# A fused attention and expert kernel: a new instruction list, sums of four v tokens fetched by an accumulating DMA, and stores issued by SyncE

## The chip, the cores and the metric

One core of one Trainium2 chip runs the kernel. The metric is device time in microseconds. The kernel before took 366.23 us when the change was made (median of three runs, 365.46 to 369.69). Its engines are called as in the profile: PE is TensorE, DVE is VectorE, ACT is ScalarE, POOL is GpSimd, and SP is SyncE. PEld is the loading of weights, which overlaps PE (183.8 us busy beside PE's 351.5 in a span of 367.9).

## The reference

Two kinds of attention are added over 8 batches, 8 heads, 576 tokens and 64 dimensions. One runs over q, k and v averaged by fours and is repeated to full length; the other runs over a band of 7 tokens. The sum, 4608 tokens by 512, goes through a dense pair of products with ELU between.

```python
q_d = q.reshape(B, H, Sd, factor, D).mean(axis=3)      # factor = 4; k_d, v_d alike
out_d = sm_attn(q_d, k_d, v_d)
out_up = np.repeat(out_d, factor, axis=2)
mask = np.abs(pos[:, None] - pos[None, :]) < factor
scores = np.where(mask, scale * q @ k.T, -1e9)          # softmax, then @ v
x = (out_up + out_local)                                # (4608, 512)
h = x @ w_in                                            # (4608, 2048), first product
g = np.where(h > 0, h, np.exp(np.minimum(h, 0)) - 1)
out = g @ w_out                                         # (4608, 512), second product
```

## The kernel before

The kernel is a list of short words, each of which issues some instructions, in an order that was worked out beforehand. Each engine runs its own share of the words in the order of the list. `mm1.t.f` is one block of four matmuls of the first product (0.87 us from start to start). `e`, `m` and `g` are its exponential on ScalarE, its minimum and its final sum on VectorE. `mm2` is the second product, `Tq` and `Tk` turn q and k, `M` multiplies by the band's mask on VectorE, `MUL` scales attention by its denominators on VectorE, `X` adds the two attentions on GpSimd, `C` casts on GpSimd, `L` loads, and `st` stores.

```python
def vsum_mm(b, j, to):                   # averages of 4 v tokens, on TensorE
    for c in range(NB):                  # 6 matmuls
        nc.tensor.matmul(to[0:KG, c // 3, :], at_once("VR")[:, ...], v16[:, c, :, :], ...)
def turn(n, b, j):
    ...                                  # cut
    if n == "q":
        vsum_mm(b, j, to[:, :, GW : GW + 128])
def v_away(b, j):                        # VD: VectorE copies them out of PSUM
    nc.vector.tensor_copy(out=vd[:], in_=x[0:KG])
def masked(b, j):                        # M
    nc.vector.tensor_tensor(out=mex[:], in0=pex[:], in1=mk2, op=AB.mult)
def elu_min(t, fc):                      # m: both operands in SBUF
    nc.vector.tensor_scalar(out=e[:], in0=e[:], scalar1=1.0, scalar2=-1.0,
                            op0=AB.min, op1=AB.add)
def elu_add(t, fc):                      # g: one operand in PSUM
    nc.vector.scalar_tensor_tensor(out=gts[t][:, fc, :], in0=hps[(t, fc)][:], scalar=0.0,
                                   op0=AB.max, in1=els.pop((t, fc))[:], op1=AB.add)
def x_add(b, j, t):                      # X: nearly all on GpSimd
    eng.tensor_tensor(out=xts[t][...], in0=ln[:, a:z], in1=_rep4(gn[...]), op=AB.add)
def store(t, tt):
    nc.scalar.dma_start(out=out[r : r + 128, :], in_=oss.pop((t, tt))[:])
```

The softmax here doesn't subtract the row's maximum and nothing guards it: scores larger than these inputs give would overflow.

## Time and profile before

| | before |
|---|---|
| median time | 366.23 us |
| profiled execution | 369.72 us, span 367.9 us, mean granted clock 0.986 |
| TensorE busy / idle | 351.5 / 16.4 us |
| VectorE busy | 239.7 us, 65% |
| GpSimd busy | 120.4 us, 33% |

The time of an execution is some 1.8 us above the span of its core (here 369.72 - 367.9).

### The profile page before, as it was taken

Reading aid. Unit: us, or ns where it says so; the run is one execution under the profiler, and the core shown is the slowest. Engines: PE = TensorE matmul, PEld = TensorE weight load, DVE = VectorE, ACT = ScalarE, POOL = GpSimd, SP = SyncE. Lnnn points to the kernel's source line nnn. Section 1 sums busy time; section 2 is a strip of 40 time slices with the busy share of each in tenths; the row PEclk is TensorE's granted clock in tenths of the full one; section 3 lists DMA queues with packets and bytes.
Section 4 is the critical chain, followed back from the end, with each engine's and each line's share of the span. In section 5 each row is a group of like instructions: output and inputs, shape, how many; then the busy total and the mean of one; then the engine's idle time right before and its main releaser. Section 6 shows DMA issues by size and latency. Waiting matters only on the chain.

```text
span 367.9 us, 9507 instructions
## 1 busy us (share of the span) xinstructions
PE 351.5 (96%) x3953; PEld 183.8 (50%) x3953; DVE 239.7 (65%) x472; ACT 208.4 (57%) x395; POOL 120.4 (33%) x177
## 2 busy tenths in 40 slices
PE   7888989899999999999999999999999999999996
PEld 3554454444555565554555545564544444444442
DVE  2856986429897548777797667887674765565520
ACT  2844883448768768377657564768363334344321
POOL 6676224361175122562292308410500410000000
PEclk9998999699999999999999999999999999999999
DMA  7999999999839959499649861112104010010012
GB/s 265 206 201 198 197 197 192 196 199 196 137 74 229 166 126 193 95 182 180 140 112 199 192 118 56 41 47 68 59 32 110 29 60 29 29 59 29 29 59 86
DMA packets 106917, 46.08 MB, mean 125 GB/s; under 512 B 92314, under 2 KB 101178, under 8 KB 106874
## 3 DMA queue, kind: packets, MB, share of 16 engines
q1 hardware_dynamic: 91402, 25.17, 40.2%
q10 hardware_dynamic: 8896, 13.36, 12.3%
q0 software_dynamic: 6576, 6.94, 11.0%
q8 instruction: 31, 0.51, 0.6%
q14 instruction: 12, 0.10, 0.1%
HBM read 42.49 MB, written 9.53 MB: 141 GB/s over the span
## 4 chain that ended last, share of the span: by engine, by line
PE 76%; DMA 8%; ACT 5%; DVE 3%; issue 3%; SPq 2%; ACTq 1%; POOL 1%; POOLq 0%
PE op L679 32%; PE hp L635 28%; DMA v<-in_v_dram 7%; PE lg L584 3%; PE sc L476 2%; SPq L316 2%; DVE gt L669 2%; PE den L539 2%; ACT e L660 2%; PE tq L369 1%; PE tq L392 1%; PE tk L392 1%; DVE e L664 1%; DMA q<-in_q_dram 1%; PE lg L590 1%
## 5 line engine op out<-in xcount | busy, mean ns | idle before, releaser
L635 PE MATMUL hp<-xt,WI 128*128 128x512 f16 x576 | 143.7, 381 | 2.3 <-DVE gt L669 2.0
L679 PE MATMUL op<-WO,gt 128*128 128x512 f16 x576 | 142.0, 384 | 0.4 <-DVE gt L669 0.3
L660 ACT ACTIVATE e<-hp 128x512 f16<-128x512 f32 x144 | 85.9, 601 | 76.0 <-PE hp L635 70.4
L669 DVE SCALAR_TENSOR_TENSOR gt<-hp,e 128x512 f16<-128x512 f32 x144 | 99.2, 690 | 4.7
L679 PEld LDWEIGHTS <-gt 128*128 128x128 f16 x576 | 53.6, 98 | 63.1 <-issue 1.8
L635 PEld LDWEIGHTS <-WI 128*128 128x128 f16 x576 | 53.3, 98 | 61.7 <-issue 5.0
L664 DVE TENSOR_SCALAR e<-e 128x512 f16<-128x512 f16 x144 | 51.5, 359 | 48.9 <-ACT e L660 48.1
L627 POOL TENSOR_TENSOR xt<-ln,gn 128x64 f16<-128x64 f16 (+7 forms) x63 | 41.8, 685 | 68.1 <-DVE ln L614 67.7
L686 ACT COPY os<-op 128x512 f32<-128x512 f32 x36 | 21.1, 587 | 41.9 <-PE op L679 41.8
L502 ACT ACTIVATE pex<-sc 112x576 f16<-112x576 f32 x64 | 41.0, 648 | 5.5 <-PE sc L486 4.2
L359 POOL CAST v<-v 112x768 f16<-112x768 f32 x30 | 24.8, 838 | 40.8 <-PE lg L584 22.7
L521 DVE TENSOR_TENSOR mex<-pex,MASK 112x1152 f16<-112x1152 f16 x32 | 25.7, 802 | 13.8 <-ACT pex L502 13.7
L354 POOL CAST q<-q 96x768 f16<-96x768 f32 x20 | 16.8, 842 | 31.0 <-issue 21.2
L508 ACT ACTIVATE dex<-sc 72x288 f16<-72x288 f32 x64 | 25.5, 405 | 1.5 <-PE sc L486 1.5
L354 POOL CAST k<-k 96x768 f16<-96x768 f32 x20 | 17.4, 876 | 26.3 <-PE tk L392 20.6
L417 ACT CAST qt<-tq 128x720 f16<-128x720 f32 x20 | 15.2, 761 | 11.5 <-PE tq L369 7.9
L476 PEld LDWEIGHTS <-kt 64*112 64x112 f16 x384 | 13.1, 127 | 14.0 <-issue 10.0
L476 PE MATMUL sc<-qt,kt 64*112 64x96 f16 x384 | 16.9, 217 | 2.1 <-ACT kt L412 0.6
L369 PEld LDWEIGHTS <-VR 112*72 112x72 f16 x192 | 13.0, 113 | 7.2 <-ACT qt L412 2.9
L614 DVE TENSOR_TENSOR ln<-lg,rcb 128x576 f16<-128x576 f32 x20 | 15.0, 748 | 0.0
L584 PEld LDWEIGHTS <-v 112*64 112x64 f16 x384 | 10.4, 111 | 7.8 <-issue 5.7
L450 DVE CAST vd<-tq 72x256 f16<-72x256 f32 x20 | 8.3, 415 | 8.8 <-ACT qt L417 8.7
(64 smaller groups left out, 273.8 us busy)
## 6 DMA issues: line engine op xcount, KB each, us to landing
v<-in_v_dram SPq DMA_DIRECT2D x28, 336.0 KB, 7.3
out_dram<-os ACTq DMA_DIRECT2D x36, 256.0 KB, 2.5
q<-in_q_dram SPq DMA_DIRECT2D x24, 288.0 KB, 5.1
k<-in_k_dram SPq DMA_DIRECT2D x24, 288.0 KB, 6.5
rcb<-rd ACTq DMA_DIRECT2D x10, 360.0 KB, 5.2
WI<-in_moe_w_in_dram POOLq DMA_DIRECT2D x4, 512.0 KB, 11.5
WO<-in_moe_w_out_dram POOLq DMA_DIRECT2D x4, 512.0 KB, 16.8
q<-in_q_dram POOLq DMA_DIRECT2D x4, 288.0 KB, 11.1
```

Source lines behind the costliest of these rows:

```text
L354: nc.gpsimd.tensor_copy(out=t, in_=x.rearrange("p (e c d) -> p c e d", e=2, d=D))
L359: nc.gpsimd.tensor_copy(out=t[:], in_=st32.pop(("v", b, j)).rearrange("p (e c) d -> p c e d", e=2))
L476: nc.tensor.matmul(sc[e][0:KW, c // 3, QB * (c % 3) : QB * (c % 3) + QB], kt[r, QB * c : QB * c + KW], q_of(b, j, r, c), start=True, stop= ...
L502: nc.scalar.activation(out=stS[(b, j)][2][:, e, :].rearrange("p (g u) -> p g u", g=2), in_=scs[(b, j)][e][0:KW, :, 0:HB], func=AF.Exp, sca ...
L508: nc.scalar.activation(out=stS[(b, j)][1][:, e], in_=scs[(b, j)][e][0:KG, :, HB : HB + SD], func=AF.Exp, scale=SCALE / 16.0,)
L521: nc.vector.tensor_tensor(out=mex[:], in0=pex[:], in1=mk2, op=AB.mult)
L627: eng.tensor_tensor(out=xts[t][:, j, t0 - TBLK * t : t1 - TBLK * t], in0=ln[:, a:z], in1=_rep4(gn[:, a // 4 : z // 4]), op=AB.add,)
L635: nc.tensor.matmul(hps[(t, fc)][:], WI[:, dc, 128 * fc : 128 * fc + 128], xts[t][:, dc, :], start=(dc == 0), stop=(dc == DMC - 1),)
L660: nc.scalar.activation(out=e[:], in_=hps[(t, fc)][:], func=AF.Exp)
L664: nc.vector.tensor_scalar(out=e[:], in0=e[:], scalar1=1.0, scalar2=-1.0, op0=AB.min, op1=AB.add)
L669: nc.vector.scalar_tensor_tensor(out=gts[t][:, fc, :], in0=hps[(t, fc)][:], scalar=0.0, op0=AB.max, in1=els.pop((t, fc))[:], op1=AB.add,)
L679: nc.tensor.matmul(ops[(t, tt)][:], gts[t][:, fc, 128 * tt : 128 * tt + 128], WO[:, fc, :], start=(fc == 0), stop=(fc == FCN - 1),)
```

## The change

The intent is to take the averages of v off TensorE for batches 3 to 7. GpSimd fetches two of every four tokens and then adds the other two by a DMA that accumulates; VectorE adds the two halves. The stores go to SyncE's queue, so that ScalarE never stands behind one. The list was worked out anew, with a floor for TensorE's use in the form of dummy matmuls (32 where there were 25). The list is changed nearly everywhere, so it is cut. One more thing goes with it: the fetched tokens and attention's results (`lg32`) share two tiles of double width, where the results had four of single width.

```diff
+V4, STORE_SP = (3, 4, 5, 6, 7), True
 ORDER = """ ... every line differs, cut ... """
+    ind[:, 52:104] = 4.0 * ind[:, 0:52]          # sums in place of averages
+        return sb.tile([128, 2 * RW], FP32, tag="lg32", bufs=2, name="lg32")   # in wide()
+    def load_v4(h, b, i):                        # U (h=0) and V (h=1)
+        nc.gpsimd.dma_start(out=st4[(b, i, "all")], in_=bass.AP(...),
+            **({"accum_op": AB.add} if h else {}))
-        if n == "q":
+        if n == "q" and b not in V4:
             vsum_mm(b, j, to[:, :, GW : GW + 128])
 def v_away(b, j):
+        if b in V4:
+            nc.vector.tensor_tensor(out=vd[:], in0=x[:, :, 0], in1=x[:, :, 1], op=AB.add)
+            ...
+            return
-        t = lg32[(b, j)] = sb.tile([128, RW], FP32, tag="lg32", bufs=4, name="lg32")
+        ...                                      # cut: halves of the tiles of wide()
-        nc.scalar.dma_start(out=out[r : r + 128, :], in_=oss.pop((t, tt))[:])
+        eng = nc.sync if STORE_SP else nc.scalar
+        eng.dma_start(out=out[r : r + 128, :], in_=oss.pop((t, tt))[:])
```

## The prediction

> **What bounds the kernel now.** I read the page top down: the engines' shares, the slices, the chain that ended last. Then stretches of 3 us where the slices dip, and the timelines of TensorE (PE) and ScalarE (ACT) there.
>
> ```profile
> PE 351.5 (96%) x3953; PEld 183.8 (50%) x3953; DVE 239.7 (65%) x472; ACT 208.4 (57%) x395; POOL 120.4 (33%) x177
> ...
> PE   7888989899999999999999999999999999999996
> ...
> PEclk9998999699999999999999999999999999999999
> DMA  7999999999839959499649861112104010010012
> ...
> PE 76%; DMA 8%; ACT 5%; DVE 3%; issue 3%; SPq 2%; ACTq 1%; POOL 1%; POOLq 0%
> ```
>
> PE is busy 96% of 367.9 us and carries 76% of the chain: from about 75 us on it is a full pipe, and every matmul taken out there shortens the run by its spacing. The other 16.4 us (367.9 - 351.5) are idle: about 1.5 at the start, 3.7 behind the last matmul (copy and store of the last tile), and about 11 nearly all before 90 us. Busy is not full speed: the granted clock falls to 0.6 in the eighth slice. The stretches there say more:
>
> ```profile
> core 0: us, PE busy (x) PEld busy (x) DVE busy (x) ACT busy (x) POOL busy (x), PEclk, DMA share, GB/s
> ...
> 60.00:63.00 3.00, 3.00 (x55) 1.66 (x54) 1.98 (x5) 0.59 (x1) 2.69 (x5) 1.00 1.09 166
> 63.00:66.00 3.00, 0.59 (x4) 0.10 (x2) 0.04 (x1) 0.71 (x2) 2.72 (x4) 1.00 1.24 179
> 66.00:69.00 3.00, 2.99 (x42) 1.65 (x44) 2.45 (x4) 1.10 (x2) 0.00 (x0) 0.70 1.18 244
> 69.00:72.00 3.00, 3.00 (x28) 1.31 (x25) 0.97 (x2) 0.82 (x3) 0.57 (x2) 0.50 1.26 172
> 72.00:75.00 3.00, 3.00 (x27) 1.44 (x28) 0.75 (x1) 1.22 (x2) 3.00 (x4) 0.66 1.36 176
> ```
>
> PE stands 2.4 us, then runs 9 us at clocks of 0.70, 0.50 and 0.66, which loses 3 x (0.30 + 0.50 + 0.34) = 3.4 us more. ACT's timeline gives the cause:
>
> ```profile
> 60.36 0.59 ACT L686 COPY os<-op 128x512 f32<-128x512 f32 x1 [1.75 <-PE op L679]
> 64.86 0.38 ACTq L690 DMA_DIRECT2D out_dram<-os  x1
> 65.28 0.64 ACT L412 CAST qt<-tq 128x576 f16<-128x576 f32 x1 [4.34 <-DMA v<-in_v_dram]
> ```
>
> The copy of an output tile ends at 60.95, its store is issued only at 64.86, and the cast that PE needs comes behind it in ACT's order. The wait is put down to a load of v[...]. DMA is saturated here (share 1.24). So PE's only large stall is a store that holds up ACT.
>
> [...] The kernel before has no accumulating DMA; no trace shows its price yet. In the built program the second half does wait for the first.
>
> **The change, part by part.**
>
> *Sums of v off TensorE.* For batches 3 to 7, 20 head pairs lose six matmuls each against the averaging matrix, 120 in all. The group list prices them at 10.0 us, the wrong figure to use[...]. The spacing is what the pipe loses:
>
> ```profile
> 155.55 0.49 PE L392 MATMUL tq<-I,q 96*128 96x120 f16 x6
> 155.87 0.50 PE L369 MATMUL tq<-v,VR 112*72 112x128 f16 x6
> 156.21 1.03 PE L679 MATMUL op<-WO,gt 128*128 128x512 f16 x4
> ```
>
> A burst shows 0.50 us but the next starts 156.21 - 155.87 = 0.34 us later; three others in the trace (at 161.83, 165.54, 178.52) give 0.33 to 0.34. 0.335/6 = 56 ns each, so 20 x 0.335 = 6.7 us come off the path. The later matmuls keep count and shape: the factor 4 between sum and mean goes into a second set of indicator columns for the denominators.
>
> *What takes their place.* VectorE's copy of the sums out of PSUM (20 x 415 ns) becomes an add of two SBUF halves of 256 elements. From this engine's rows 748 ns for 576 elements and 303 for 144, that is 155 + 1.03 x 256 = about 420 ns (estimate): no change for DVE. GpSimd issues 20 more DMAs; its DMA rows read 0.7 to 0.8 us, so 15 us more on an engine busy 33%. Each brings 72 x 8 x 512 bytes = 295 KB, 5.9 MB in all. Today's hardware queue takes 40.2% of 367.9 us for 25.17 MB, 5.9 us of all engines per MB, so 35 us of DMA time[...]. Between 100 and 260 us the eight stretches of 20 us have shares 0.76, 0.76, 0.72, 1.03, 0.74, 0.83, 0.15, 0.24: 105 us used, against about 200 at the 1.25 seen when saturated. It fits, without much room in the middle.
>
> *Stores by SyncE.* ACT no longer queues behind a store. The stall of 2.4 us and the slow clock after it (3.4 us) should go: 5.8 us. The cost: SyncE works in order, so a store waiting for its copy holds up the loads behind it. Ten load buffers give slack; I charge nothing. The store at the very end takes the same path by another queue: no change.
>
> *The list.* "A floor for PE's use" shows as fillers: 32 dummy matmuls in place of 25, all early, seven more at 0.216 us = 1.5 us if they stood on the path; most will lie in idle time, so I charge 0.5. In return the clock's dip at 24 to 30 us (0.87 and 0.56 over two 3 us stretches, 0.4 + 1.3 = 1.7 us) should shrink; I count 0.9. Of the small idles before 60 us (about 6 us besides the start) I count 1.0 saved.
>
> *New waits.* The second half can be issued only when the first has landed, and VectorE's add waits for the second. By the list most adds stand 8 us or more behind their accumulate; for three (second half of batch 3, second of batch 4, first of batch 5) only five or six blocks of four matmuls, about 0.87 us each start to start, lie between: 4 to 6 us. Loads of this size land thus today:
>
> ```profile
> v<-in_v_dram SPq DMA_DIRECT2D x28, 336.0 KB, 7.3
> ...
> q<-in_q_dram SPq DMA_DIRECT2D x24, 288.0 KB, 5.1
> ...
> q<-in_q_dram POOLq DMA_DIRECT2D x4, 288.0 KB, 11.1
> ```
>
> With 6 to 9 us for an accumulate (estimate), the three would hold VectorE for 1 to 4 us each, of which PE feels perhaps a third, since hidden tiles are double-buffered and the second product's matmuls go on: +2.5 us.
>
> *Sum:* -6.7 - 2.4 - 3.4 - 0.9 - 1.0 + 0.5 + 2.5 = -11.4 us. From 366.2: 354.8, say 355.
>
> **The rivals.** First, the accumulate is slow (over 10 us to land): GpSimd waits in order for first halves, its casts come late, VectorE stands at the adds, and PE starves in batches 3 to 5 by some us per batch. For it: no accumulating DMA has been seen here, and GpSimd's own loads took 11 us. Against: those ran in saturated DMA. It would give back the 6.7 us and leave 360 to 364. Second, the stall at 61 us merely moves: DMA is saturated to about 90 us, and data that is not there stays so whoever issues the store; the reordered loads could stop PE elsewhere, with another dip of the clock. For it: a DMA share above 1.2 from 10 to 70 us. Against: during the stall GpSimd was busy 2.7 of 3 us, and PE lacked only ACT's cast of data already in PSUM. It would give 359 to 361. Third, everything goes well: no new waits, clock at 1.00 and half of the early idle gone: about 350. A fourth, that PE's work is hidden anyway and taking it out gains nothing, has 96% busy against it.
>
> **Range and chances.** The 6.7 us are the firm part; the 5.8 us of the stall I hold at 80%; the new waits are uncertain by 5 us. So 355, with 350 to 361 to hold it 8 times in 10. The 2% line below is 366.2 x 0.98 = 358.9: missing it needs the stall to stay or a slow accumulate, so 0.82 faster, 0.16 within 2%, 0.02 slower.
>
> **What would show it.** Right: no VR matmuls into tq; 72 into vs remain; PE busy 7 to 10 us less by the page's count; no gap of 2 us on PE near 60 us, no slice of the clock at 6, mean clock above 0.986; no wait of ACT on a load of v. Issue to landing of the accumulates at 6 to 9 us; DMA slices fuller from 100 to 250 us. Wrong: DVE or GpSimd waiting for DMAs of v for several us in batches 3 to 5 with PE idle behind them; a new stall before 90 us with a slow clock after it; SyncE's stores holding loads that PE then lacks.

## More of the kernel before

The prediction shows most of the lines of this profile. It leaves out three rows of the costliest groups, VectorE's largest. Their columns are the line, the engine, the operation, the operands and the count, then busy us and mean ns of one, then the idle time ahead of them and what ended most of it.

```profile
L669 DVE SCALAR_TENSOR_TENSOR gt<-hp,e 128x512 f16<-128x512 f32 x144 | 99.2, 690 | 4.7
...
L664 DVE TENSOR_SCALAR e<-e 128x512 f16<-128x512 f16 x144 | 51.5, 359 | 48.9 <-ACT e L660 48.1
...
L521 DVE TENSOR_TENSOR mex<-pex,MASK 112x1152 f16<-112x1152 f16 x32 | 25.7, 802 | 13.8 <-ACT pex L502 13.7
```

What counts below is the mean of one. One `g` takes 690 ns and one `m` 359 ns on the mean, though most of the `m` in the timelines take 290 ns.

## The result, and the profile after

The changed kernel took 378.35 us (median of four runs, 376.71 to 381.94). The kernel before took 365.85 us beside it. The ratio is 1.033, with a 95% interval of 1.023 to 1.043: slower. A ratio here is the mean time of one kernel's fast runs over the mean of the other's of the same rounds, so it is not quite the ratio of the medians. All ratios below are to the kernel before, and 0.01 is 3.66 us.

The page of the changed kernel, its line of engines, the slices of TensorE and of its clock, and the chain that ended last:

```profile
PE 345.9 (92%) x3840; PEld 177.2 (47%) x3840; DVE 255.1 (68%) x472; ACT 208.4 (55%) x395; POOL 143.5 (38%) x197
...
PE   7898879978888988889979999999999999999996
...
PEclk9999999999999999999998999999999999999999
...
PE 64%; DVE 14%; DMA 12%; ACT 5%; issue 2%; POOL 1%; SPq 1%; DVEq 0%; ACTq 0%
```

The slow clock at 65 to 75 us (6 tenths in the eighth slice of the kernel before, 9 here) is gone, as was predicted. But TensorE's idle time is 376.3 - 345.9 = 30.4 us, where it was 16.4. It lies in slices that were full before: where the kernel before has nines from the ninth slice on, this one has mostly eights up to the 21st, which ends at 198 us, and a seven in the 24th. VectorE's share of the chain rose from 3% to 14%.

VectorE got 15.4 us more busy time (255.1 - 239.7) with the same 472 instructions. The rows of the groups that answer to the three above:

```profile
L700 DVE SCALAR_TENSOR_TENSOR gt<-hp,e 128x512 f16<-128x512 f32 x144 | 99.1, 691 | 4.7
L695 DVE TENSOR_SCALAR e<-e 128x512 f16<-128x512 f16 x144 | 62.4, 435 | 57.9 <-ACT e L691 57.1
...
L549 DVE TENSOR_TENSOR mex<-pex,MASK 112x1152 f16<-112x1152 f16 x32 | 29.3, 914 | 12.4 <-ACT pex L530 12.3
```

The `g`, with one operand in PSUM, costs the same (691 ns against 690). The `m` and the mask product, with all operands in SBUF, cost 62.4 - 51.5 = 10.9 us and 29.3 - 25.7 = 3.6 us more. The timeline shows how that happens. Columns: start, duration, engine and line, and in brackets the idle time just before and who ended it.

```profile
73.95 0.82 POOL L376 CAST q<-q 96x768 f16<-96x768 f32 x1
...
74.36 4.62 DVE L549 TENSOR_TENSOR mex<-pex,MASK 112x1152 f16<-112x1152 f16 x1
...
74.74 1.31 POOL L658 TENSOR_TENSOR xt<-ln,gn 128x128 f16<-128x128 f16 x2
...
77.54 0.82 POOL L376 CAST q<-q 96x768 f16<-96x768 f32 x1
78.90 0.74 DVE L478 CAST vd<-vs 72x256 f16<-72x256 f32 x2
...
79.36 0.79 PE L504 MATMUL sc<-qt,kt 64*112 64x96 f16 x12 [2.61 <-DVE vd L478]
```

A mask product that takes 0.76 us elsewhere (the median) took 4.62 us. During it GpSimd ran six instructions without a gap, until 77.54 + 0.82 = 78.36; the product ended at 78.98, and TensorE had stood 2.61 us for the short copies behind it. The same is seen at 192.87 us, where an `m` lasted 3.12 us while GpSimd ran without a gap and TensorE then stood 2.39 us. The trace shows which instructions are stretched, and beside what. Of the `m` and mask products of the changed kernel, 39 took more than 10 ns over their usual 0.29 and 0.76 us, and every one of the 39 ran beside a GpSimd instruction. The 95 `m` that had none beside them took 0.30 us at most. Counted so, the stretching adds up to 26.3 us in the changed kernel and to 11.7 us in the kernel before. Eight `m` had only the issue of a DMA by GpSimd beside them: these took 0.36 us on the mean and 0.46 at most. The `g` show no stretching: 39 of them also ran beside a GpSimd instruction, and took 0.69 us on the mean and at most.

### The profile page after: what moved, and what is told of

It reads as the page before. It is cut to its first block, busy times and chain, and to the rows that moved or that the text cites.

```text
span 376.3 us, 9363 instructions
## 1 busy us (share of the span) xinstructions
PE 345.9 (92%) x3840; PEld 177.2 (47%) x3840; DVE 255.1 (68%) x472; ACT 208.4 (55%) x395; POOL 143.5 (38%) x197
## 3 DMA queue, kind: packets, MB, share of 16 engines
q0 software_dynamic: 15536, 12.88, 21.3%
## 4 chain that ended last, share of the span: by engine, by line
PE 64%; DVE 14%; DMA 12%; ACT 5%; issue 2%; POOL 1%; SPq 1%; DVEq 0%; ACTq 0%
PE op L710 30%; PE hp L666 25%; DMA v<-in_v_dram 10%; DVE e L695 5%; DVE gt L700 3%; DVE ln L645 3%; PE sc L504 2%; ACT e L691 2%; PE lg L613 2%; DVE mex L549 1%; ACT pex L530 1%; PE den L568 1%; PE tq L414 1%; DMA q<-in_q_dram 1%; DMA MASK<-MASKc 1%
## 5 line engine op out<-in xcount | busy, mean ns | idle before, releaser
L666 PE MATMUL hp<-xt,WI 128*128 128x512 f16 x576 | 142.2, 380 | 8.1 <-DVE gt L700 7.9
L710 PE MATMUL op<-WO,gt 128*128 128x512 f16 x576 | 139.8, 381 | 3.2 <-DVE gt L700 3.2
L695 DVE TENSOR_SCALAR e<-e 128x512 f16<-128x512 f16 x144 | 62.4, 435 | 57.9 <-ACT e L691 57.1
L549 DVE TENSOR_TENSOR mex<-pex,MASK 112x1152 f16<-112x1152 f16 x32 | 29.3, 914 | 12.4 <-ACT pex L530 12.3
L381 POOL CAST v<-v 112x768 f16<-112x768 f32 x30 | 26.5, 884 | 23.0 <-DMA v<-in_v_dram 22.1
L359 POOL DMA_DIRECT2D lg<-in_v_dram x20 | 23.1, 1181 | 25.5 <-DMA lg<-in_v_dram 19.4
L376 POOL CAST q<-q 96x768 f16<-96x768 f32 x20 | 18.9, 944 | 23.1 <-PE tq L414 14.5
L376 POOL CAST k<-k 96x768 f16<-96x768 f32 x20 | 19.2, 983 | 6.0 <-PE tk L414 4.4
L442 ACT CAST kt<-tk 128x576 f16<-128x576 f32 x20 | 12.9, 645 | 3.4 <-PE tk L414 3.4
## 6 DMA issues: line engine op xcount, KB each, us to landing
WO<-in_moe_w_out_dram POOLq DMA_DIRECT2D x4, 512.0 KB, 16.7
```

What stands on the lines that cost most here:

```text
L376: nc.gpsimd.tensor_copy(out=t, in_=x.rearrange("p (e c d) -> p c e d", e=2, d=D))
L381: nc.gpsimd.tensor_copy(out=t[:], in_=st32.pop(("v", b, j)).rearrange("p (e c) d -> p c e d", e=2))
L666: nc.tensor.matmul(hps[(t, fc)][:], WI[:, dc, 128 * fc : 128 * fc + 128], xts[t][:, dc, :], start=(dc == 0), stop=(dc == DMC - 1),)
L710: nc.tensor.matmul(ops[(t, tt)][:], gts[t][:, fc, 128 * tt : 128 * tt + 128], WO[:, fc, :], start=(fc == 0), stop=(fc == FCN - 1),)
```

## The experiments

Eighteen runs were made. Each is told with its edit, as far as it is not the list. "The old list" is the list of the kernel before, and "the new list" that of the changed kernel.

| run | list | sums of v by | stores by | median us | ratio (95%) |
|---|---|---|---|---|---|
| e1_old_sp | old | TensorE | SyncE | 364.84 | 0.997 (0.991 to 1.002) |
| e3_new_nov4 | new | TensorE | SyncE | 381.53 | 1.040 (1.035 to 1.046) |
| e5_new_nofetch | new | constant, VectorE adds | SyncE | 375.75 | 1.026 (1.021 to 1.031) |
| changed kernel | new | DMA, VectorE adds | SyncE | 378.35 | 1.033 (1.023 to 1.043) |
| e11_new_noadd | new | constant, no add | SyncE | 379.39 | 1.024 (1.016 to 1.032) |
| e7b_old_nofetch | old | constant, VectorE adds | SyncE | 364.38 | 0.991 (0.985 to 0.997) |
| e7c_old_noadd | old | constant, no add | SyncE | 360.45 | 0.986 (0.981 to 0.990) |
| e14_old_v67 | old | DMA in batches 6, 7 | SyncE | 362.54 | 0.989 (0.985 to 0.993) |

### The stores alone

The first run takes the change of stores into the old list, with nothing else.

```diff
 def store(t, tt):
-        nc.scalar.dma_start(out=out[r : r + 128, :], in_=oss.pop((t, tt))[:])
+        nc.sync.dma_start(out=out[r : r + 128, :], in_=oss.pop((t, tt))[:])
```

> Old list and old arithmetic, only the 36 stores by SyncE. If the prediction was right on this part, ScalarE no longer stands at 61 us, TensorE's 2.4 us gap and the slow clock after it are gone, and the time falls by 5 to 6 us to about 360. Rival: SyncE, which works in order, makes loads wait for copies (and stores for load buffers), and the gain goes: 364 to 369.

It took 364.84 us, 0.997 of the kernel before, an interval that holds 1. In its profile the stall at 61 us and the slow clock behind it are gone (no slice of the clock is below 9 tenths from the fifth on), and the span is 362.6 us where that of the kernel before was 367.9. But that 5.3 us is the difference of two profiled executions. The kernel before was therefore profiled again.

> The kernel before, profiled once more, because its first profile was of an execution of 369.7 us where the median is 366. If the 2.4 us stall at 61 us and the slow clock after it are of every execution, they show again. If they are the accident of that one execution, the span is 363 to 365 us, with no gap over 1 us near 61 us, and the 5.8 us that the prediction took off for them were never to be had.

It was a long execution again: 370.09 us, clock 0.986, with the stall and the slow clock in the same place: TensorE is busy 1.45 of 3 us at 63 to 66 us, and the clock is 0.85, 0.50 and 0.51 in the next three stretches of 3 us. The medians of the timed executions lie near 366 us. So the stall is real where it is seen, but its removal is worth 1.3 us by the ratio in the timed executions, not 5.8. Whether the shorter executions lack the stall, or lose elsewhere what SyncE's stores save, is not shown.

Given back to ScalarE within the changed kernel, the stores are another matter.

```diff
-V4, STORE_SP = (3, 4, 5, 6, 7), True
+V4, STORE_SP = (3, 4, 5, 6, 7), False
```

> The changed kernel with the stores given back to ScalarE's queue. By the prediction's sum (5.8 us for the stores) it would be slower than the changed kernel by some 6 us: 384. By what e1_old_sp showed in the old list (1.7 us in the median, within the interval of zero): 377 to 381.

It took 396.35 us, with two of four runs slow; the fast ones are at 1.070 (1.060 to 1.079), 0.037 or 13 us above the changed kernel. Both expectations were too small. Its profile, of a slow execution, has the old stall in a larger form, ScalarE behind a load of v and TensorE behind ScalarE (6.7 us). The lines of the waits give the total, the count and the longest:

```profile
ACT lg L630 <- DMA v<-in_v_dram: 7.3, 1, 7.3
```

So the move to SyncE is worth 13 us in the new list and 1.3 us in the old one.

### The list alone

The next run is the counterpart: the new list with the old arithmetic, the sums on TensorE and no fetch. The words for the fetches are taken out, and VectorE's copy stands right behind the turn of q.

```diff
-V4, STORE_SP = (3, 4, 5, 6, 7), True
+V4, STORE_SP = (), True
 ORDER = """ ... U and V words dropped, VD words behind Aq ... """
```

> New list and SyncE's stores, but no second fetch of v: the sums are made on TensorE again (each copy to VectorE right behind its turn). If the 20 fetches and GpSimd's waits on them cause the loss between 100 and 210 us (14 us more lag of TensorE than before), the 6.7 us of TensorE work come back and some 12 us go: about 373, with VectorE's stretched instructions falling from 28 us to about 15. If the new list itself causes it, about 385.

It took 381.53 us, 1.040. Beside e1, on the same chip, the list differs, and the double-width tiles: 381.53 - 364.84 = 16.7 us, or 16.0 by the ratios. This is the largest effect, and none of the new arithmetic is in it. Nor is it the tiles, or a list that misses the arithmetic it was made for. Two pairs below have the tiles and the new arithmetic without fetches on both sides, and differ in the list alone: e11 and e7c, 1.024 against 0.986, are 14 us apart, and e5 and e7, 1.026 against 0.995, are 11 us apart. So the list costs 11 to 16 us.

Where TensorE waits in e1:

```profile
PE hp L635 <- DVE gt L669: 2.1, 5, 0.7
...
PE op L679 <- DVE gt L669: 0.3, 1, 0.3
...
PE vs L369 <- POOL v L359: 0.2, 1, 0.2
```

and in the changed kernel:

```profile
PE hp L666 <- DVE gt L700: 7.9, 9, 1.4
PE op L710 <- DVE gt L700: 3.2, 2, 2.4
PE sc L504 <- DVE vd L478: 2.6, 1, 2.6
PE vs L391 <- POOL v L381: 2.3, 2, 1.2
```

All the lines of this view add up to 9.0 us in e1 and 25.7 us in the changed kernel, which is 16.7 us more. That is also the growth of TensorE's idle time, 30.4 against 362.6 - 348.9 = 13.7. Of it, waits put down to VectorE make 18.7 - 4.8 = 13.9 us, GpSimd 2.1, and ScalarE 1.0. In e3 the waits for VectorE are 12.7 us, so 7.9 of these 13.9 come with the list alone. e3's profile is not typical, though: its clock is 0.976, from slices at 0.6 and 0.5 behind groups of waits, and TensorE's idle time in it grew by only 10.6 us (381.7 - 357.4 against 13.7). Its other three executions have 0.996 to 1.000 and 379 to 382 us, so the clock is not the cause of the loss.

Stretching is not the cause in e3 either. VectorE is busy 238.1 us there, no more than before, and its `m` and mask products are stretched by 11.6 us in all, as in the kernel before (11.7):

```profile
PE hp L662 <- DVE gt L696: 8.5, 11, 1.6
...
L691 DVE TENSOR_SCALAR e<-e 128x512 f16<-128x512 f16 x144 | 50.3, 351 | 57.2 <-ACT e L687 56.5
...
L545 DVE TENSOR_TENSOR mex<-pex,MASK 112x1152 f16<-112x1152 f16 x32 | 26.6, 832 | 13.6 <-ACT pex L526 13.5
```

So in e3 it is not longer instructions but the places of VectorE's work in the list, and what waits behind it, that can account for the 7.9 us.

The timeline of e3 shows one place:

```profile
109.47 1.47 DVE L691 TENSOR_SCALAR e<-e 128x512 f16<-128x512 f16 x1
...
111.72 1.02 PE L662 MATMUL hp<-xt,WI 128*128 128x512 f16 x4 [0.76 <-DVE gt L696]
...
112.67 1.51 DVE L691 TENSOR_SCALAR e<-e 128x512 f16<-128x512 f16 x1
...
114.96 1.87 PE L662 MATMUL hp<-xt,WI 128*128 128x512 f16 x4 [1.56 <-DVE gt L696]
```

The hidden tile has two buffers, so a block of the first product waits for the `g` of the block before the last. For each block VectorE needs 0.29 + 0.69 = 0.98 us, and TensorE 0.87. The order has to put other work of TensorE between blocks, and no other work of VectorE. Here the list sets all four `MUL` of batch 2 (0.30 + 0.75 us of VectorE each) around two blocks of the first product and two of the second. The old list spreads them over four of the first product and one of the second. And GpSimd's additions, which the `MUL` release, run right beside the `m`, which takes 1.5 us.

A list that is old up to about 111 us and new behind it asks which half hurts.

```diff
 ORDER = """ ... the old list up to X2.2.3, then the new one's remaining words ... """
```

> Old list up to the last block of the first product of tile 1 (some 110 us), the new list from there on, with the fetches. If the new list loses mostly in its first 130 us (8 us more lag there than the old list with SyncE's stores), 378 falls to about 370. If it loses mostly behind, where the fetches are: 376 to 379.

It took 383.04 us, 1.045 (1.038 to 1.053), worse than either list and outside both expectations. The join itself has a hole: in the two slices from 104 to 123 us TensorE is busy 5 and 7 tenths, at a clock of 8 and 5 tenths. That leaves TensorE idle for about 6 to 8 us (an estimate from the digits, at 9.5 us a slice), as much as the good first half could have saved, so this run decides nothing. That the new list loses behind 111 us too is said by the changed kernel's trace: from 140 to 160 us TensorE is busy 17.0 of 20 us where it had 19.4.

### Is it VectorE?

Four runs take work away from VectorE. Their outputs are wrong, which doesn't matter for the times. The first drops the `m` from the changed kernel, 62 us of VectorE, and the second does so in e1 as a control.

```diff
 def elu_min(t, fc):
-        nc.vector.tensor_scalar(out=e[:], in0=e[:], scalar1=1.0, scalar2=-1.0, ...)
+        del e
```

> The changed kernel without VectorE's 144 min-and-add instructions on the exponentials (wrong on purpose), which takes 62 us off VectorE and its slowest link with TensorE. If the new list loses its time where VectorE's pace of 0.98 us a block holds TensorE's 0.86, the time falls to 360 us or below. If the loss is elsewhere (ScalarE, GpSimd, waits for data), it stays at 372 or above.

> The control for e9_new_nomin: the old list with stores by SyncE, without the same 144 instructions (wrong on purpose). In the old list VectorE hides beside TensorE, so by the theory of VectorE's pace it gains little: 361 to 365 us. If it gains as much as e9 does, then taking 62 us off VectorE shortens any list and says nothing on the new one.

In the new list the median was 372.66 us; two of four runs were over 1.5% above the fastest, and the fast two (367.72 and 370.16) make 1.017 (1.007 to 1.027), 0.016 or 6 us below the changed kernel. The old list gained 0.010: 362.84 us, 0.987 (0.980 to 0.993). So the wait for `g` was real, and it falls from 11.1 to 1.9 us in the trace, but the time did not fall to 360. Dropping the `m` doesn't take the rest of VectorE's queue away, and the mask product at 74 us still lasts 4.6 us. The expectation of the theory was too bold.

The next two have no fetch and no add of v sums either: VectorE has nothing in place of the copies.

```diff
 def v_away(b, j):
-            nc.vector.tensor_tensor(out=vd[:], in0=x[:, :, 0], in1=x[:, :, 1], op=AB.add)
-            stV[(b, j)][1] = vd
+            stV[(b, j)][1] = BUSY[0:KG, 0:256].rearrange("p (k d) -> p k d", d=D)
```

> The changed kernel without fetches and without VectorE's 20 adds (wrong on purpose; e5_new_nofetch had the adds and took 375.8). If TensorE waits for VectorE in the new list, some 10 us of VectorE work less give 369 to 373 us; if the order holds TensorE by other waits, it stays at 374 to 376.

> As e11_new_noadd and without the 144 min-and-add instructions of VectorE too (wrong on purpose). If VectorE were all of the new list's loss: 358 to 361 us, the 362.8 of e10_old_nomin less part of the 6.7 us. If there is a rest that is not VectorE's: 364 to 370, and the waits of TensorE for ScalarE and for loaded data name it.

The adds' removal gave nothing in the new list: 379.39 us (372.84 to 381.62), the fast two at 1.024, beside e5's 1.026. This speaks against the adds as the load that matters there. But VectorE was not relieved by all of it: its `m` and mask products were stretched by 23.3 us in this trace, against 12.4 in e7c, the same work in the old list. Removal of the `m` on top gave 367.19 us, the fast two (362.15 and 366.18) at 0.994 (0.987 to 1.002): 0.030 or 11 us less than e11. In the old list the same 144 instructions gave 0.010. VectorE's pace thus carries 2 to 7 us of the new list's loss (0.016 - 0.010 and 0.030 - 0.010). What is left, about 0.994 against what an old list without all this should give (0.986 - 0.010 = 0.976, an estimate), is 7 us. For it the trace offers only waits: 2.6 us behind the long mask product, 4.8 us behind ScalarE's exponentials of scores, 1.4 us behind a cast. These kernels also scatter by about 2% from run to run, and each ratio rests on two fast runs, so the sizes are rough.

The long mask product could be tested by itself. One word moves in the list, the mask product `M2.1`, so that the two short copies `VD2.3` and `VD2.0` come first.

```diff
-VS2.3 M2.1 oc.0.2 VS2.0 Lq3.1 mm2.0.12 VD2.3 Cq3.0 st.0.2 VD2.0 mm2.0.13 X1.3.2 ...
+VS2.3 oc.0.2 VS2.0 Lq3.1 mm2.0.12 VD2.3 Cq3.0 st.0.2 VD2.0 M2.1 mm2.0.13 X1.3.2 ...
```

> The changed kernel with one pair of places swapped: VectorE's two short copies of token sums (0.41 us each) go ahead of the mask product of batch 2, which took 4.62 us between GpSimd's gap-free operations at 74 us and behind which TensorE stood 2.6 us. Correct result. If the order of VectorE's work is what hurts there, the gap of TensorE before the scores at 77 us falls from 2.6 us to under 0.7, and the time by about 2 us, to 375 to 377. If TensorE stood for something else, the gap stays at 2 us or more.

It took 375.52 us with a correct result, 1.023 (1.017 to 1.029), which is 2.8 us less by the medians; the intervals overlap. The mask product is still stretched, but nothing waits behind it:

```profile
74.55 0.78 DVE L476 CAST vd<-vs 72x256 f16<-72x256 f32 x2 [0.27 <-PE vs L389]
...
75.24 3.55 DVE L547 TENSOR_TENSOR mex<-pex,MASK 112x1152 f16<-112x1152 f16 x1
...
76.52 0.51 PE L502 MATMUL sc<-qt,kt 64*112 64x96 f16 x12
```

TensorE's scores start without a wait, where they had one of 2.61 us. The place of one word thus cost 2.6 us of TensorE's time, and by the medians about a quarter of the 12.5 us by which the changed kernel is slower: the list held a stretched instruction ahead of short ones that TensorE needed.

### What the sums of v are worth

Three runs without the fetches measure what the matmuls taken off are worth. The first is in the new list: VectorE adds halves of a constant tile, and the fetches are gone (wrong).

```diff
 def load_v4(h, b, i):
+        t = once[0][0:KG, 0:1024].rearrange("p (g h d) -> p g h d", h=2, d=D)
+        for n in range(2):
+            st4[(b, 2 * i + n)] = t[:, 4 * n : 4 * n + 4]
+        return
```

> The changed kernel without its 20 fetches: VectorE's add reads a tile set once, so the result is wrong on purpose; TensorE's saving and the list stay. If the fetches cause the loss after 100 us: about 365 (378 less 13). If the list does: 375 to 378.

It took 375.75 us, 1.026. Against e3 the matmuls are worth 0.014 or 5.1 us in the new list. The fetches then add 0.007 or 2.6 us, which is within the noise, as the intervals overlap. The constant tile is set on VectorE in this run, 1.26 us at 112 us; no wait of TensorE ends on it in the trace, and e11, which has no such setting, gave 1.024. The same in the old list:

> Old list, SyncE's stores, 120 averaging matmuls gone and no fetch (VectorE adds a tile set once; wrong result on purpose). The price of the first term alone: against the 364.8 of the old list with SyncE's stores, 6.7 us less, 358. If TensorE's work there is hidden: 363 to 365.

The first try, 364.61 us and 0.995, had an accident: my setting of the constant tile on VectorE, 1.26 us at 104 us, made TensorE stand 3.0 us. It was repeated with a tile that exists from the start.

```diff
-            nc.vector.memset(once[0][:], 0.5)
+        t = BUSY[0:KG, :].rearrange("p (g h d) -> p g h d", h=2, d=D)
```

> The old list with stores by SyncE, the averaging matmuls of batches 3 to 7 taken out, no fetch by GpSimd, and VectorE adding two halves of a constant tile in their place (wrong on purpose); this repeats e7_old_nofetch without the memset that made a 3.0 us gap of its own there. If the 6.7 us of matmuls are on the path, as the prediction's first step says: 364.8 - 6.7 = 358 us (357 to 360). If something beside TensorE takes their place in this list as well: 363 to 365.

It took 364.38 us, 0.991. Against e1 that is 0.005 or about 2 us, with intervals that overlap, and not 6.7. Its windows, TensorE first and the granted clock third from the end, show where 3.4 us of the saving went:

```profile
100.00:103.00 3.00, 3.00 (x23) 1.57 (x24) 2.96 (x5) 2.43 (x6) 1.80 (x4) 1.00 0.31 64
103.00:106.00 3.00, 1.35 (x12) 0.75 (x10) 3.00 (x5) 1.07 (x2) 2.95 (x5) 1.00 0.80 183
106.00:109.00 3.00, 2.87 (x18) 1.60 (x17) 2.18 (x6) 1.48 (x3) 0.00 (x0) 0.67 0.06 13
109.00:112.00 3.00, 3.00 (x19) 1.43 (x17) 1.77 (x4) 2.16 (x5) 2.67 (x4) 0.76 0.00 0
```

VectorE is busy all of 103 to 106 us: an `m` of 2.06 us and an add of 0.90 us, both stretched beside GpSimd, which was busy 2.95 of 3 us. TensorE, which now came earlier, waited 1.65 us for it, and its clock then fell to 0.67 and 0.76, another 3 x (0.33 + 0.24) = 1.7 us. In e1 the same place has no wait. So TensorE's saving seems to have been met by VectorE. If so, it must come back when the add is gone as well:

> As e7b_old_nofetch (old list, stores by SyncE, no averaging matmuls, no fetch; wrong on purpose), and VectorE's add is gone as well: the products take a constant tile at once. If VectorE is what eats the TensorE time saved in e7b, the full 6.7 us appear: 357 to 359.5 us. If the saved time is hidden behind something else: 362 to 365.

It took 360.45 us, 0.986: 0.011 or 4.0 us against e1. The time is 1 us above the expected range, so the theory holds in direction and not in full. With VectorE relieved, 4.0 of 6.7 us appear; with the add in, 2 us. The rest is lost in small waits for `g`, 3.9 us in this trace against 2.4 in e1.

### The fetches in the old list

Three kernels put the whole arithmetic of the change, fetches included, into the old list. The first two differ in their stores and in the places that I gave to the words of the fetches.

```diff
 ORDER = """ ... the old list; U and V words put in by hand, VD words moved later ... """
```

> Old list with the 20 fetches put in by hand where GpSimd was idle before, each accumulate 9 us or more behind its first half; stores by ScalarE as before. If the arithmetic is good and its placement was the trouble: 366 - 6.7 = about 359. If fetching v twice by itself costs (DMA traffic[...]): 366 or more.

> Old list, SyncE's stores, the 20 fetches of v placed with more slack: 10 to 16 us from the accumulate to its use, and away from the small DMAs that spread the reciprocals. If the 12 us that the fetches cost in the first hand-made list were waits for late landings, now 365 - 6.7 = 358 to 360. If DMA traffic or the GpSimd time costs in itself: 364 or more.

> The old list with stores by SyncE and the 20 fetches of summed tokens, placed a second time so that none stands in front of GpSimd's additions to x (correct result). If the fetches are cheap once nothing waits for them: 358 + 2.5 = 360 to 362 us, which would beat both kernels. If they cost in themselves whatever the list: 365 or more.

The first took 371.93 us, 1.012 (1.006 to 1.018). VectorE waited 5.0 us for an accumulate, and a small transfer by ScalarE took 8.1 us and held ScalarE. The second took 372.81 us, 1.016: no wait for an accumulate, but a fetch that I had put ahead of GpSimd's additions made TensorE stand 5.8 us. The third took 370.82 us, 1.010 (1.004 to 1.016), with 4.4 us of TensorE behind a return load of denominators that I had moved too late. Each has a wait of its own making, so these three do not say what fetches cost at their best. They say that in the busy middle of this list three tries by hand found no place where 20 fetches pay.

The last run keeps them to where GpSimd, the DMA queues and VectorE have room: batches 6 and 7, behind 200 us. In the trace of the kernel before, in the four stretches of 20 us from 200 to 280 us, GpSimd is busy 3.3 to 12.6 us and VectorE 13.3 to 16.8, and the DMA share is 0.83, 0.15, 0.24 and 0.16.

```diff
-V4, STORE_SP = (3, 4, 5, 6, 7), True
+V4, STORE_SP = (6, 7), True
 ORDER = """ ... the old list, U and V for batches 6 and 7 only ... """
```

> The old list with stores by SyncE, and the summed tokens by GpSimd's accumulating DMA only in batches 6 and 7 (correct result): 8 head pairs lose 8 x 0.335 = 2.7 us of matmuls, after 200 us, where DMA and GpSimd have room. If the saving counts there: 362 to 363.5 us, 0.99 of the kernel before. If it is eaten there too: 364.5 to 366.

It took 362.54 us with a correct result (six runs, 361.03 to 364.19), 0.989 (0.985 to 0.993), clear of 1. This is the fastest correct kernel, faster than both by 1.1% and 4%. TensorE's idle time in its trace is 362.4 - 349.1 = 13.3 us, where e1 has 13.7: the fetches brought no new wait. Beside e1 it gained 0.0075 or 2.7 us, which is just the 8 x 0.335 us of the matmuls; the intervals of the two runs overlap, so the match of the sizes is better than the evidence for it.

## Why the prediction was wrong, point by point

**The step that failed is "The list".** It was priced as fillers (+0.5), a smaller dip of the clock (-0.9) and some idle time (-1.0), together -1.4 us. Measured, the list costs +16.7 us with the old arithmetic (e3 against e1), and 11 to 14 us in the two pairs that differ in nothing else. By the ratios the steps from the kernel before to the changed one are -1.3 us for the stores (e1), +16.0 for the list (e3), -5.1 for the matmuls (e5) and +2.6 for the fetches. The prediction read the list for its dummy matmuls and for the distance between a fetch and its use. It did not ask, block by block, what VectorE had to do between two hidden tiles. It took 96% of TensorE as a property of the kernel, when it was one of the old order. Between the traces of e1 and the changed kernel TensorE's idle time grew by 16.7 us, and waits for VectorE are 13.9 of them. In the time, VectorE's pace carries 2 to 7 us by the runs without the `m`, and the place of one mask product about 2.8.

**Bound.** That TensorE sets the time was right for the kernel before. "Every matmul taken out there shortens the run by its spacing" was not: with nothing in their place (e7c) the 120 matmuls were worth 4.0 us, with VectorE's add (e7b) 2 us, in place of 6.7. VectorE, at 65% over the whole, is busy 3.00 of 3 us just where it counts (103 to 106 us in e7b). The fourth rival, that TensorE's work is hidden anyway, was dismissed by the 96%; it held in part.

**Sums off TensorE.** The count was right (3840 matmuls are 120 fewer and 7 fillers more than 3953). The price of 6.7 us came out at 5.1 in the new list (e5 against e3). TensorE's busy time fell by 5.6 us, where the prediction's signs had 7 to 10.

**"No change for DVE".** The add's estimate of 420 ns was right, as the changed kernel's median is 412 ns. But VectorE's busy time grew by 15.4 us, 14.5 of it in the stretched `m` and mask products. The prediction counted instructions and took their durations from the kernel before. The list with the old arithmetic shows no such growth (238.1 us in e3). It comes when the averaging matmuls are gone, even without a fetch (an `m` takes 391 ns in e5 and 406 in e11), and is largest with the fetches (435), which keep GpSimd busy with 23.1 us of issue.

**GpSimd's issue and the landing.** The issue was put at 15 us and took 23.1. The landing was put at 6 to 9 us and took 7.9. Told apart by their order in the list, the ten accumulating halves held GpSimd 1.39 us each at the median and landed after 8.1 us (5.7 to 12.0); of the ten plain halves eight held it 0.84 to 0.89 us, near the 0.7 to 0.8 that the prediction had read. The DMA time was put at 35 us: GpSimd's queue took 21.3% of 376.3 = 80.2 us of all engines, where it took 11.0% of 367.9 = 40.5, so 39.7 us more. The group row and the row of DMA issues of the changed kernel:

```profile
L359 POOL DMA_DIRECT2D lg<-in_v_dram x20 | 23.1, 1181 | 25.5 <-DMA lg<-in_v_dram 19.4
...
lg<-in_v_dram POOLq DMA_DIRECT2D x20, 288.0 KB, 7.9
```

**New waits.** +2.5 us fits in size, as the fetches cost 2.6 us (the changed kernel against e5, within the noise), by luck, as it was wrong in kind. VectorE never waited for an accumulate in the changed kernel. GpSimd waited 19.4 us for first halves and ran what had gathered afterwards, and VectorE's `m` took 62.4 us where they took 56.1 in e5. That the one led to the other is a reading of the trace.

**Stores by SyncE.** The stall was seen rightly, and it went away with the stores, clock and all. But 5.8 us was read from an execution 3.5 us longer than the median; the gain was 1.3 us by the ratio (e1), within an interval that holds zero. In the new list the same move is worth 13 us (e2), which the prediction had no means to see. SyncE did stand for copies: 217.0 us in all ahead of its 36 stores in the changed kernel, 11.3 at most. A load that came next in its order was issued right behind, as the load of q at 117.68 us behind the store at 117.22. What that cost was not measured apart.

**The rivals.** The slow accumulate did not come, nor did the stall move while SyncE stored. None of the four named the order as the danger, and the range ended at 361.

What stays open: some 7 us of the new list's loss are named by waits only, and not tested by taking each away. That the stretching is GpSimd's doing rests on the count above (39 of 39); no run took GpSimd's work away to prove it.

## What to carry to other kernels

A list that was worked out anew is a change of its own, and here the largest: run it once with the old arithmetic before crediting or blaming anything else in the change. Check, where two engines hand tiles to and fro over two buffers, whether the second engine's work per tile, at its stretched duration, is below the first's; a share over the whole run doesn't show it. And before pricing a stall from a profile, compare the profiled execution with the median of the timed ones.

## What the traces show of the engines

- VectorE beside a row of GpSimd instructions: a mask product of the changed kernel lasted through six of them without a gap, 4.62 us in place of 0.76, and ended 0.62 us behind the last; an `m` took 3.12 us in place of 0.29.
- The price of accumulation: the issue of an accumulating half held GpSimd 1.37 to 1.46 us, where eight of ten plain halves took 0.84 to 0.89, and the landing took 5.7 to 12.0 us, 8.1 at the median, where a plain half took 6.5, for 288 KB each.
- TensorE's clock after a wait: one wait of 1.65 us on a busy stretch was followed by 0.67 and 0.76 (e7b), and in the changed kernel one of 2.39 us by 0.73 and 0.70 (196 to 202 us), but one of 2.61 us by 1.00 (80 to 83 us). Among these three the length of the wait did not decide it.
